# A convolution of three taps by points: inputs laid out ahead, output kept transposed, and the transform of x done channel block by channel block with two points of two output blocks among it

## The chip, the core and the metric

The kernel runs on one core of a Trainium2 chip. The metric is the device time of one execution in microseconds. It has four compute engines that run beside each other: TensorE (PE; its weight loads are shown as PEld), VectorE (DVE), ScalarE (ACT) and GpSimd (POOL). SyncE (SP) issues most of the DMA transfers here. TensorE writes into PSUM, of which there are eight banks of 512 fp32 values per partition; VectorE and ScalarE read it.

## The reference

x is (2, 2048, 1024), w is (3, 1024, 1024), all in bf16; the four parameters have 1024 values each.

```python
xp = jnp.pad(x, ((0, 0), (P, P), (0, 0)))          # P = 1
y = sum(jnp.einsum('bsc,cd->bsd', xp[:, k:k + S, :], w[k]) for k in range(K))   # K = 3
inv_std = 1.0 / jnp.sqrt(var + 1e-5)
y = (y - mean) * (g * inv_std) + b
return _silu(y)
```

It is a convolution along the sequence with three taps, a full product over 1024 channels for each tap, a batch norm with given mean and variance, and a silu.

## The kernel before, in words

Both kernels compute six neighbouring rows of the output from eight rows of the input by way of eight points (0, three pairs of plus and minus, and infinity). Per batch the 2048 rows make NB = 342 groups of R = 6. Three things have to be made from the data: the transform of x, called T (for each batch, channel block of 128 and point a tile of 128 channels x 342 groups), the transform of the weights (for points 1 to 6, the tiles u; points 0 and infinity use taps 0 and 2 of the weights as they are), and, for each batch and each of the eight output blocks of 128 channels, eight products of 8 matmuls each, which are then combined to six output rows.

**Transform of x.** x comes in as windows of 128 rows by 1024 channels (`load_x`, L119; 17 a batch, overlapping by two rows; 21 groups to a window, 6 in the last). TensorE multiplies a window's 128 channels with the matrix rm (L322): the result is already transposed, channels on partitions, 8 points x 21 groups = 168 columns. A job (`t_job`, L314) does up to three channel blocks of two windows into two PSUM banks, and one eviction casts the 1008 (or 672) columns a partition to bf16 in T (ScalarE L333 or VectorE L335). There are 24 such jobs a batch and one small one. At build time a small cost model (`clock`, `cost`, L106) gives each eviction to the engine that it thinks will end sooner. Batch 0's jobs run first, with four pairs of banks in turn (`ahead`, L604); batch 1's jobs are put between the matmuls of the first unit (class `Between`, L622), on the pairs at banks 4, 6 and 1.

**Units.** A unit is one output block of one batch (class `Unit`, L344). It holds four banks, 0 to 3 or 4 to 7, in turn. `run` (L473) issues the products of points 1, 3, 2, 4, 5, 6 (L369); after products 1, 3, 2 and 5 ScalarE copies a bank out (L380, L382), on which the next product into that bank waits; VectorE combines PSUM and the copies (L387). The products of point 0 and of infinity need nothing but T and the raw taps and are added onto two of the banks at the end. They (`first`, L400, `last`, L405) and the silus (L394) of one unit run inside the next one, behind its fifth and its sixth product (`rest`, L465, and the hook `behind`, L477). 16 units, dc by dc and batch by batch; the last one is done in two halves of the columns, 214 and 128 groups.

**Weights.** GpSimd adds and subtracts (L188, L167, L243), VectorE or ScalarE make the multiples by 2 and 4 (L169, L155, L237); `prepare_first`, `prepare_second` and `prepare_w` (L206, L230, L190) for output blocks 0, 1 and the others. The loads take 128 or 256 columns of a row of w at a time (L139).

**Matrix and parameters.** rm is made by some twenty small VectorE instructions (L77 to L102), the parameters are loaded as rows and transposed by TensorE (L282), and GpSimd makes scale and beta of them (L285 to L295).

**Output.** The silus leave yT, channels on partitions. `turn` (L572) sends it through a DMA transpose on SP and `store` (L581) writes rows of 128 channels. For the last two units TensorE transposes instead (`put`, L519, L530), VectorE or ScalarE copy out of PSUM (L531).

Each DMA on SP's queue waits for the eighth before it to have landed; a load into a tile waits also for its last reader.

Of the kernel before, what the change touches and what calls it, by code (L numbers as in the profile page):

```python
# [12 lines left out]
I32 = mybir.dt.int32  # L13
ENG = mybir.EngineType

P = 128
R = 6
NJ = 8
W0_AT = (5, 8, 16)
EARLY = 23  # L20
XBUFS = 12
T_FIRST = 21500.0
WARM = 2
WT = 21

@with_exitstack
def kernel(
    ctx: ExitStack,
    tc: tile.TileContext,
    x: bass.AP,  # L30
    w: bass.AP,
    mean: bass.AP,
    var: bass.AP,
    g: bass.AP,
    b: bass.AP,
# [3 lines left out]
    B, S, C = x.shape  # L39
    D = w.shape[2]  # L40
    CT, DC = C // P, D // P
    NB = -(-S // R)
    NW = -(-NB // WT)
    LAST = NB - WT * (NW - 1)
    assert S % P == 0 and NB <= 512
# [3 lines left out]
    wpool = ctx.enter_context(tc.tile_pool(name="wpool", bufs=1))  # L49
# [7 lines left out]
    opool = ctx.enter_context(tc.tile_pool(name="opool", bufs=2))  # L57
    xwin_scope = ExitStack()
    xpool = xwin_scope.enter_context(tc.tile_pool(name="xpool", bufs=XBUFS))
# [8 lines left out]
    rows = consts.tile([4 * DC, P], BF16, name="rows")  # L68
# [8 lines left out]
    def transform_matrix():  # L77
        v = nc.vector
        val = consts.tile([P, 3, WT], I32, name="val")
        nc.gpsimd.iota(val, pattern=[[1, 3], [-R, WT]], base=-1, channel_multiplier=1)  # L80
        m = consts.tile([P, 4, 3, WT], FP32, name="m")
        f = consts.tile([P, 3, 2, WT], FP32, name="f")
        c = consts.tile([P, 2, WT], FP32, name="c")
        rm = consts.tile([P, NJ, WT], BF16, name="rm")
        m0, m2, m4, m6 = (m[:, q] for q in range(4))
        for q, coef in ((1, -8.0), (2, 1.0), (3, 1.0), (0, 36.0)):
            v.tensor_scalar(m[:, q], val, float(2 * q), coef, op0=ALU.is_equal, op1=ALU.mult)
        for k, (c4, c6) in enumerate(((34.0, -8.0), (40.0, -32.0), (10.0, -2.0))):
            v.scalar_tensor_tensor(out=f[:, k], in0=m4[:, 1:3], scalar=c4, in1=m2[:, 1:3], op0=ALU.mult, op1=ALU.add)
        v.scalar_tensor_tensor(out=c, in0=m6[:, 0:2], scalar=-36.0, in1=m0[:, 0:2], op0=ALU.mult, op1=ALU.add)  # L90
        for k, (c4, c6) in enumerate(((34.0, -8.0), (40.0, -32.0), (10.0, -2.0))):
            v.scalar_tensor_tensor(out=f[:, k], in0=m6[:, 1:3], scalar=c6, in1=f[:, k], op0=ALU.mult, op1=ALU.add)
        v.scalar_tensor_tensor(out=c, in0=m4[:, 0:2], scalar=189.0, in1=c, op0=ALU.mult, op1=ALU.add)
        f1, f2, f3 = (f[:, k] for k in range(3))
        for j, a0, s0, a1, op in (
            (1, f1[:, 0], 1.0, f1[:, 1], ALU.add), (2, f1[:, 0], 1.0, f1[:, 1], ALU.subtract),
            (3, f2[:, 1], 2.0, f2[:, 0], ALU.add), (4, f2[:, 1], -2.0, f2[:, 0], ALU.add),
            (5, f3[:, 0], 2.0, f3[:, 1], ALU.add), (6, f3[:, 0], 2.0, f3[:, 1], ALU.subtract),
            (0, m2[:, 1], 23.625, c[:, 1], ALU.add), (7, m2[:, 0], -23.625, c[:, 0], ALU.subtract),
        ):  # L100
            v.scalar_tensor_tensor(out=rm[:, j], in0=a0, scalar=s0, in1=a1, op0=ALU.mult, op1=op)
        return rm  # L102

    rm = transform_matrix()

    clock = {"pe": 3500.0, "act": 0.0, "dve": 0.0, "dma": 3600.0}  # L106
    cost = {"act": (0.833, 250.0), "dve": (1.042, 215.0)}
    bank_free = {}

    def ends(e, size):  # L110
        return max(clock[e], clock["pe"] + 100.0) + cost[e][0] * size + cost[e][1]

    def busy(e, size):
        clock[e] = ends(e, size)

    order = [NW - 1] + list(range(2, NW - 1)) + [0, 1]
    xwin = {}

    def load_x(bi, wi):  # L119
        xw = xpool.tile([P, C], BF16, name="xw")  # L120
        lo = max(R * WT * wi - 1, 0)
        hi = min(lo + P, S)
        nc.sync.dma_start(out=xw[0:hi - lo, :], in_=x[bi, lo:hi, :])  # L123
        clock["dma"] += 5.4 * (hi - lo)
        xwin[bi, wi] = xw, clock["dma"]

    w_all = w.rearrange("k (ct p) d -> p k ct d", p=P)
    raw, wts = {}, {}

    wpools = {0: wpool}  # L130

    def load_w(pair, k, half=None):

        if (pair, "tile") not in raw:
            raw[pair, "tile"] = wpools[pair % 2].tile([P, 3, CT, 2, P], BF16, name=f"wch{pair % 2}")
        wch = raw[pair, "tile"]
        h0, h1 = (0, 2) if half is None else (half, half + 1)
        cols = slice((2 * pair + h0) * P, (2 * pair + h1) * P)
        nc.sync.dma_start(  # L139
            out=wch[:, k, :, h0:h1].rearrange("p c h d -> p c (h d)"), in_=w_all[:, k, :, cols]  # L140
        )
        clock["dma"] += 1400.0 * (h1 - h0)
        for h in range(2):
            raw[2 * pair + h] = wch[:, :, :, h]
# [200 lines left out]

# [382 lines left out]
```

## Time and profile before

| what | value |
|---|---|
| time, median of 3 runs | 187.73 us (187.33 to 187.81) |
| span of the profiled execution, first to last instruction | 185.5 us |
| time of the profiled execution beside its span | not given on the page |
| PE, DVE, ACT, POOL busy | 178.0, 153.0, 112.9, 146.8 us |
| products (L369) | 1088 matmuls: 960 of 342 columns, 64 of 214, 64 of 128 |
| windows of x (L322) | 272 matmuls, 256 of 168 columns |
| first window matmul, first product | 5.2 us, 19.6 us |
| last window matmul starts | 37.2 us |

How to read it: the page lists each engine's busy time, the span in 40 slices of 4.64 us, the chain of work that ended last, and the costliest groups of instructions. A group's line has the source line, the engine, what is written and read, the shape, the count, then busy microseconds and the mean length of one in nanoseconds, then the idle time ahead of them and who ended it. "L369" is a line of the kernel above. In the timeline and the chain, the first number is the start from the beginning of the span and the second the length, in microseconds.

### The profile page before, as it was taken

To read this page: it belongs to the slowest core of one execution; us is meant where nothing else is said; L and a number is where in the kernel's file an instruction comes from. 1 tells how busy PE (TensorE), PEld (TensorE's weight loads), DVE (VectorE), ACT (ScalarE), POOL (GpSimd) and SP (SyncE) were. 2 spreads that over 40 slices of the span, in tenths; PEclk is the share of its full clock that TensorE was granted. 3 is DMA by queue.
4 is the path that set the end of the run, shared out by engine and by line. 5 is a ranking of instruction groups with operands and counts; after the bars stand their busy time and mean duration, and the time that the engine had idled before them with its cause. 6 is when DMAs were issued, how large, how long until landed. Compare 5 with 4: busy or idle time off the path is not lost.

```text
span 185.5 us, 3732 instructions
## 1 busy us (share of the span) xinstructions
PE 178.0 (96%) x1403; PEld 125.9 (68%) x1403; DVE 153.0 (82%) x214; ACT 112.9 (61%) x183; POOL 146.8 (79%) x89
## 2 busy tenths in 40 slices
PE   6889999999999999999999999999999999999991
PEld 2678688866666666666666666666666666669890
DVE  5278777997668999999988998879988997678792
ACT  3589888896638565456545654565456546363791
POOL 7099899999998879999999999999999973020120
PEclk9999999999999999999999999999999999999998
DMA  5999999065426855698859557995583968766845
GB/s 166 326 344 328 377 386 252 7 203 143 79 48 62 183 106 134 198 200 187 161 114 206 109 135 156 217 211 108 136 178 80 209 57 203 151 139 134 196 96 113
DMA packets 88046, 31.72 MB, mean 171 GB/s; under 512 B 75659, under 2 KB 83866, under 8 KB 88028
## 3 DMA queue, kind: packets, MB, share of 16 engines
q1 hardware_dynamic: 86860, 31.24, 72.3%
q10 hardware_dynamic: 848, 0.20, 0.5%
q8 instruction: 11, 0.18, 0.4%
q0 software_dynamic: 320, 0.03, 0.2%
q14 instruction: 7, 0.06, 0.1%
HBM read 14.82 MB, written 8.39 MB: 125 GB/s over the span
## 4 chain that ended last, share of the span: by engine, by line
PE 85%; DMA 5%; DVE 4%; ACT 2%; SPq 1%; issue 0%; DVEq 0%; ACTq 0%
PE ps L369 79%; DMA xw<-in_x_dram 5%; PE ps L322 5%; DVE T_sb L335 3%; SPq L123 1%; ACT T_sb L333 1%; PE ps L530 1%; DVE sd L387 0%; DVE o L531 0%; ACT outer L394 0%; DVEq L335 0%; ACTq L333 0%
## 5 line engine op out<-in xcount | busy, mean ns | idle before, releaser
L369 PE MATMUL ps<-T_sb,u 128*128 128x342 bf16 (+2 forms) x816 | 120.1, 299 | 0.1
L369 PEld LDWEIGHTS <-u 128*128 128x128 bf16 x816 | 76.8, 97 | 33.4 <-issue 0.2
L188 POOL TENSOR_TENSOR u<-e,w1x 128x1024 bf16<-128x1024 f32 x32 | 69.4, 2191 | 3.9 <-DVE e L169 2.5
L369 PE MATMUL ps<-T_sb,wch 128*128 128x342 bf16 (+2 forms) x272 | 42.6, 299 | 0.4 <-ACT T_sb L333 0.4
L394 ACT ACTIVATE yT<-ps,beta,scale 128x342 bf16<-128x342 f32 (+4 forms) x49 | 33.5, 713 | 13.3 <-PE ps L369 13.3
L387 DVE SCALAR_TENSOR_TENSOR t<-ps,sd 128x684 f32<-128x684 f32 (+2 forms) x51 | 39.1, 822 | 0.6
L188 POOL TENSOR_TENSOR u<-e,wch 128x1024 bf16<-128x1024 f32 x16 | 38.5, 2424 | 1.2 <-DMA wch<-in_w_dram 0.7
L369 PEld LDWEIGHTS <-wch 128*128 128x128 bf16 x272 | 25.7, 97 | 11.9 <-issue 0.6
L380 ACT COPY pc<-ps 128x342 f32<-128x342 f32 (+2 forms) x35 | 14.9, 426 | 28.7 <-PE ps L369 28.4
L333 ACT CAST T_sb<-ps 128x1008 bf16<-128x1008 f32 (+2 forms) x31 | 25.6, 874 | 7.4 <-PE ps L322 7.1
L335 DVE CAST T_sb<-ps 128x1008 bf16<-128x1008 f32 (+2 forms) x19 | 20.7, 1116 | 10.4 <-PE ps L322 10.3
L387 DVE SCALAR_TENSOR_TENSOR ps<-ps,t 128x684 f32<-128x684 f32 (+2 forms) x34 | 28.3, 832 | 0.6
L169 DVE SCALAR_TENSOR_TENSOR e<-wch 128x1024 f32<-128x1024 bf16 x12 | 26.2, 2182 | 0.0
L322 PE MATMUL ps<-rm,xw 128*128 128x168 bf16 (+2 forms) x272 | 25.0, 237 | 1.0 <-ACT T_sb L333 0.3
L322 PEld LDWEIGHTS <-xw 128*128 128x128 bf16 (+2 forms) x272 | 20.9, 100 | 6.4 <-issue 3.7
L387 DVE SCALAR_TENSOR_TENSOR ps<-ps,pc 128x342 f32<-128x342 f32 (+2 forms) x34 | 16.9, 497 | 9.2 <-PE ps L369 7.8
L167 POOL TENSOR_TENSOR e<-wch 128x1024 f32<-128x1024 bf16 x7 | 16.9, 2409 | 0.4 <-DMA wch<-in_w_dram 0.4
L394 ACT ACTIVATE yT<-t,beta,scale 128x684 bf16<-128x684 f32 (+2 forms) x17 | 15.7, 924 | 0.0
L387 DVE SCALAR_TENSOR_TENSOR t<-ps,t 128x684 f32<-128x684 f32 (+2 forms) x17 | 13.9, 818 | 0.0
L589 POOL DMA_DIRECT2D out_dram<-o x2 | 1.3, 659 | 15.6 <-DMA o<-yT 15.6
L387 DVE SCALAR_TENSOR_TENSOR sd<-pc,ps 128x342 f32<-128x342 f32 (+2 forms) x17 | 8.2, 485 | 6.2 <-ACT sd L380 6.1
L380 ACT COPY sd<-ps 128x342 f32<-128x342 f32 (+2 forms) x17 | 7.3, 428 | 9.7 <-PE ps L369 9.1
(62 smaller groups left out, 61.8 us busy)
## 6 DMA issues: line engine op xcount, KB each, us to landing
xw<-in_x_dram SPq DMA_DIRECT2D x32, 256.0 KB
out_dram<-o SPq DMA_DIRECT2D x28, 192.0 KB
wch<-in_w_dram SPq DMA_DIRECT2D x8, 512.0 KB
wch<-in_w_dram SPq DMA_DIRECT2D x8, 256.0 KB
out_dram<-o SPq DMA_DIRECT2D x14, 120.0 KB
out_dram<-o SPq DMA_DIRECT2D x3, 128.0 KB
o<-yT SPq DMA_TRANSPOSE x15
out_dram<-o SPq DMA_DIRECT2D x12, 7.5 KB
```

The costliest lines, as they stand in the source:

```text
L123: nc.sync.dma_start(out=xw[0:hi - lo, :], in_=x[bi, lo:hi, :])
L167: eng.tensor_tensor(e, w0, w2, op=ALU.add)
L169: eng.scalar_tensor_tensor(out=e, in0=f, scalar=4.0, in1=h, op0=ALU.mult, op1=ALU.add)
L188: nc.gpsimd.tensor_tensor(wts[dc, q][:, i], sums[dc, q], o, op=(ALU.add, ALU.subtract)[i])
L322: nc.tensor.matmul(v[:, q, c], lhsT=xw[0:rows, (c0 + c) * P:(c0 + c + 1) * P], rhs=mat[0:rows, :, 0:n], start=True, stop=True,)
L333: nc.scalar.copy(dst, src)
L335: nc.vector.tensor_copy(dst, src)
L369: nc.tensor.matmul(self.bank[q], lhsT=lhsT, rhs=T_sb[self.bi][:, ct, j, nsl], start=not add and ct == 0, stop=ct == CT - 1, skip_group_che ...
L380: nc.scalar.copy(dst, self.bank[q])
L387: nc.vector.scalar_tensor_tensor(out=out, in0=in0, scalar=scalar, in1=in1, op0=ALU.mult, op1=op1)
L394: nc.scalar.activation(dst, src, ACT.Silu, bias=beta[:, dc:dc + 1], scale=scale[:, dc:dc + 1])
L530: nc.tensor.transpose(v[:, a, q], src, ident)
```

## The change

The host now lays out the inputs: x as windows by channel block, (batch, block of 128 channels, 128 rows, 16 windows, 128 channels), and the rest of its rows apart (xl, 48 rows); w as (output block, 128 rows, tap, channel block, 128 columns); the parameters as columns; and the matrix rm as an input. The output is stored as it lies in yT (output block, channel, 6, 342), and the host reorders it. The building of rm, the transpose of the parameters, the DMA transposes (`turn`), the transposes by TensorE (`put`), and one of two warming matmuls are gone.

T is made channel block by channel block: a load brings one block of all 16 windows (512 KB), and its three jobs are six, six and four windows. The jobs of both batches take the pairs of banks at 4 and 6 in turn. Banks 0 to 3 hold, during batch 0's transform, the sums of points 0 and infinity for output blocks 0 and 1 of batch 0: as soon as the cost model thinks that a channel block of T is complete, its matmuls are issued among the jobs. These four sums are copied to SBUF (`ends_of`), and units 0 and 2 add them in on VectorE (two more instructions each) in place of the two products; their silus, three of 684 columns, go to places 1, 2 and 3 of the following unit. Batch 1's jobs are again put between the matmuls of the first unit, whatever is left behind its fifth product (`between.rest`). The cost model has new constants.

In the order that results, 23 of batch 0's 24 large jobs are evicted by ScalarE and one by VectorE; of batch 1's, 21 and three. Behind the first unit's fifth product there are 13 jobs left, all for ScalarE.

```diff
-T_FIRST = 21500.0
-WARM = 2
+AHEAD = 2
+XBUFS = 8
...
-    for _ in range(WARM):
-        nc.tensor.matmul(ps[:, 7], lhsT=zeros[:, 0:P], rhs=zeros, start=True, stop=True)
+    nc.tensor.matmul(ps[:, 7], lhsT=zeros[:, 0:P], rhs=zeros, start=True, stop=True)
...
-    rm = transform_matrix()
+    rm = consts.tile([P, NJ, WT], BF16, name="rm")
+    nc.scalar.dma_start(out=rm, in_=rm_in)
...
-    cost = {"act": (0.833, 250.0), "dve": (1.042, 215.0)}
+    cost = {"act": (0.833, 60.0, 200.0), "dve": (1.042, 160.0, 60.0)}
...
+    class Jobs:
+        def __init__(self, bi, banks):
+            self.bi, self.banks, self.n = bi, banks, 0
+            self.todo = [(None, 0, 0)] + [
+                (ct, f, min(6, NF - f)) for ct in range(CT) for f in range(0, NF, 6)
+            ]
...
+        def do(self):
+            clock["pe"] = max(clock["pe"], self.ready())
+            bank = self.banks[self.n % len(self.banks)]
+            self.n += 1
...
+                src = ps[:, bank:bank + 2, 0:per * NJ * WT].rearrange("p b (f j n) -> p b f j n", f=per, j=NJ)
+                for q in range(nf):
+                    nc.tensor.matmul(
+                        src[:, q // per, q % per], lhsT=xt[self.bi, ct][:, f + q], rhs=rm, start=True, stop=True
+                    )
+                src = src.rearrange("p b f j n -> p j b f n")
+                dst = T[:, ct, :, f * WT:(f + nf) * WT].rearrange("p j (b f n) -> p j b f n", b=2, f=per)
+            clock["pe"] += size / 2.3
+            e = min(("act", "dve"), key=lambda k: ends(k, size, clock["pe"]))
...
         def rest(self, between, last=5, first=6):
+            if self.ends is not None:
+                return [
+                    (1, lambda: self.silu(slice(2, 4), self.y23)), (2, lambda: self.silu(slice(0, 2), self.low)),
+                    (3, lambda: self.silu(slice(4, 6), self.high)),
+                ]
...
-            self.combine(sd[:, 1], pa, 2.0, b3, ALU.subtract)
+            self.combine(sd[:, 2], pa, 2.0, b3, ALU.subtract)
+            s0 = s5 = sd[:, 0:3:2]
+            if self.ends is not None:
+                self.combine(sd[:, 1], b3, 1.0, self.ends[:, 0])
+                self.combine(sd[:, 3], sd[:, 2], 1.0, self.ends[:, 1])
+                s0, s5 = sd[:, 1:3], sd[:, 0:4:3]
...
+    jobs = Jobs(0, (4, 6))
+    accs = [(dc, k, bank) for dc, k, bank in ((0, 0, 0), (0, 2, 3), (1, 0, 1), (1, 2, 2)) if dc < AHEAD]
...
+    while jobs or any(todo.values()):
+        best = ahead()
+        if jobs and (best is None or jobs.ready() <= max(clock["pe"], best[0])):
+            ct, f, nf = jobs.todo[0]
+            jobs.do()
+            if ct is not None and f + nf == NF:
+                complete.add((0, ct))
+        else:
+            ahead_do(best)
...
     class Between:
+        jobs = Jobs(1, (4, 6))
...
+        if i == 0:
+            second[0]()
+            also = also + [(5, between.rest)]
+        if i == 1:
+            also = [(1, second[1]), (2, second[2]), (4, second[3])] + also
...
+    h1 = Unit(dc, bi, 0, 0, H)
+    h1.run(quiet, [(3, h0.silu_inner)])
+    h0.store(sp, inner)
+    h0.product(3, NJ - 1, True, quiet)
+    h0.product(0, 0, True, quiet)
+    h1.product(0, 0, True, quiet)
+    h1.product(3, NJ - 1, True, quiet)
```

More of the change, by code (lines that the diff above doesn't have):

```diff
@@ L12 @@
 BF16 = mybir.dt.bfloat16
-I32 = mybir.dt.int32
 ENG = mybir.EngineType
@@ L127 @@
[L127 to L144, printed above, removed]
@@ L344 @@
+    yts = [ypool.tile([P, R, NB], BF16, name=f"yT{q}") for q in range(B)]
     class Unit:
@@ L677 @@
-    before.store(late)
+            second[0]()
+            also = also + [(5, between.rest)]
+        if i == 1:
+            also = [(1, second[1]), (2, second[2]), (4, second[3])] + also
+        if i == 3:
+            also = also + [(1, lambda: idle(act_work)), (1, lambda: idle(dve_work))]
+        if i == len(seq) - 2:
+            also = prev.rest(quiet, 4, 5)
+        unit.run(
+            between if i == 0 else quiet, also,
+            2 if i == 2 else dc + 2 if bi == 1 and 0 < dc < DC - 2 else None, i == 2,
+        )
@@ L705 @@
[L705 to L709 removed]
+    inner, outer = slice(1, R - 1), slice(0, R, R - 1)
+    h0 = Unit(dc, bi, 4, H, NB)
+    h0.run(quiet, prev.rest(quiet, 5, 5))
+    prev.store(sp)
+    h1 = Unit(dc, bi, 0, 0, H)
[4 more added lines that the diff above has]
+    h1.product(0, 0, True, quiet)
```

611 lines of the change are left out of this document (229 added, 382 removed), and 8 rows, old and new, of the table _POINTS.

## The prediction

> **What bounds the kernel now.** I read the page's parts 1 and 2 first, then the busy time by stretches, then the chain of work that ended last in order of time, then the groups by shape.
>
> ```profile
> PE 178.0 (96%) x1403; PEld 125.9 (68%) x1403; DVE 153.0 (82%) x214; ACT 112.9 (61%) x183; POOL 146.8 (79%) x89
> ...
> PEclk9999999999999999999999999999999999999998
> ...
> GB/s 166 326 344 328 377 386 252 7 203 143 79 48 62 183 106 134 198 200 187 161 114 206 109 135 156 217 211 108 136 178 80 209 57 203 151 139 134 196 96 113
> ```
>
> TensorE is busy 96% of the span, but a matmul's recorded time overlaps the next one, so this does not say that it issues all the time. The chain does:
>
> ```profile
> 30.27 1.22 DVE T_sb L335
> 31.49 0.04 issue
> 31.54 0.61 PE ps L322 x6
> 32.15 0.02 issue
> 32.17 1.21 DVE T_sb L335
> ...
> 37.44 136.02 PE ps L369 x952
> ...
> 180.47 0.46 PE ps L369 x8
> 180.93 0.03 issue
> 180.95 0.57 ACT outer L394
> 181.53 0.42 DVE o L531
> ```
>
> Columns: start, length, what. Two things are to be seen. From 37.44 on TensorE is the bound: 952 products in 136.02 us. 32 of them have 214 columns (0.0918 apart), which leaves 133.1 for 920 of 342 columns, **0.1447 each**. Before that the chain alternates between an eviction and the next transform: eviction over, 0.05 later six matmuls into the PSUM banks it freed (0.61), 0.02 later the eviction of those. This loop prices the change. TensorE's whole work is 1024 products of 342 columns (148.2) and the transforms (256 windows at 0.0725, 18.6, and small ones), some 167 us; the rest of the span is the wait for the first data, the waits before 37.44, and the tail.
>
> **Durations** come from the groups by shape (count, busy us and mean ns):
>
> ```profile
> L333 ACT CAST T_sb<-ps 128x1008 bf16<-128x1008 f32 x17 | 17.0, 1007 | 3.6 <-PE ps L322 3.4
> L333 ACT CAST T_sb<-ps 128x672 bf16<-128x672 f32 x13 | 9.5, 731 | 0.3 <-PE ps L322 0.2
> L335 DVE CAST T_sb<-ps 128x1008 bf16<-128x1008 f32 x15 | 17.9, 1206 | 9.0 <-PE ps L322 8.9
> L530 PE MATMUL ps<-ident,yT 128*128 128x128 bf16 x34 | 2.9, 219 | 0.0
> ```
>
> and from ScalarE's timeline:
>
> ```profile
> 37.18 1.62 ACT L333 CAST T_sb<-ps 128x1008 bf16<-128x1008 f32 x2
> ...
> 40.20 1.06 ACT L155 ACTIVATE w1x<-wch 128x1024 bf16<-128x1024 bf16 x1
> 41.16 0.45 ACT L382 ACTIVATE pc<-ps 128x342 f32<-128x342 f32 x1
> ...
> 46.15 0.95 ACT L394 ACTIVATE yT<-t,beta,scale 128x684 bf16<-128x684 f32 x1
> 47.00 0.91 ACT L394 ACTIVATE yT<-ps,beta,scale 128x684 bf16<-128x684 f32 x1
> 47.94 0.44 ACT L380 COPY pc<-ps 128x342 f32<-128x342 f32 x1
> ```
>
> The first line is a 1008 eviction and a 672 one, 1.62 together. The 672 row gives the second 0.72, so it starts 0.90 after the first began, though the first is over only after 1.00. In the same way the next instruction starts 0.61 after a 672, 0.35 after a copy of 342, 0.96 after a scaled weight (40.20 to 41.16), 0.85 or 0.94 after a silu of 684 from SBUF or PSUM.
>
> **Phase 1, the transform of batch 0.** Before, its 24 large jobs take four pairs of banks in turn, and both engines evict (over both batches ScalarE 31, VectorE 19 jobs). In the changed program, banks 0 to 3 hold the sums of points 0 and inf, so jobs have two pairs (4-5, 6-7), and its order gives all large jobs but one to ScalarE. A channel block is three jobs, A and B (1008) and C (672). Set C's eviction at 0. A reuses the pair that B left: B began 0.90 earlier and is over at 0.10; 0.05 and 0.63 later A's eviction starts, 0.79, where ScalarE was free at 0.61. B starts 0.90 after A (1.69), the next C at 2.58. So **2.58 us per block**, 20.6 for eight. The first A starts at about 4.7: the old first window starts at 5.2 behind two warming matmuls (3.78 us, half of which go), and then the first half block, 0.36 MB at the first slice's pace, sets it; 0.5 either way. The last C is over at 25.3. The 32 early products (0.145 each) fit into TensorE's waits, except the last four, behind that eviction: 26.0. The loads do not set this: 5.6 MB, of which the page's row moves 0.77 in the first slice and, at the 385 GB/s of its best slices, the rest by 17.2.
>
> **Phase 2, batch 1 with the first unit.** Till all but 13 jobs are done TensorE issues 40 products (5.8), 64 window matmuls (4.64) and 8 small ones (0.3), and is the bound: 36.7 to 36.8. Then all remaining jobs (a C and four blocks) come in one run, all on ScalarE, which begins that C at 38.1 behind a copy: 38.1 + 4 x 2.58 = 48.4 for the last C. TensorE has issued its last window at 47.8, does the first unit's sixth product (1.16), and starts the second unit at **48.9**.
>
> **What is left then.** 880 products of 342 columns (127.3), and the last unit in two column halves: 64 at 0.0918 (5.9) and 64 at 0.0559 (3.6), starts read off the trace: 136.8, so **185.7**. In the old trace this remainder begins at 42.1 (37.44 and 32 products more), with 37 transposes of 0.056 in it (2.1 us of TensorE), which the change drops. So the changed kernel is 6.8 late there and gets 2.1 back.
>
> **Pile-ups on ScalarE in units 1 and 3.** The change takes the two early products out of units 0 and 2, which so far ran inside the following unit behind its fifth product, and puts three silus of 684 there, in units 1 and 3, at ScalarE's first free places. Unit 1 has also three scaled weights ahead of its last copy. From its first copy at 50.3: 0.35, 0.96, 0.85, 0.36, 0.96, 0.94, 0.35, 0.94, 0.96, and 0.44 for the copy that its sixth product waits on: 57.4, where TensorE came to it at 54.7. Loss **2.7**. In unit 3 the same with one scaled weight: its fourth product waits 0.6 for a copy, and the sixth 0.7, since no product stands between it and the copy of the fifth: **1.3**. GpSimd does not add: its chain for block 1 (2.13 a step) is ready 1 to 2 us ahead of each product. Bounds of this part: 0, if silus and copies came in a kinder order, and 5.2, if the silus also delay VectorE's sums by the length of one more silu.
>
> **Tail.** The second half's products take 0.45 each, its first copy waits for the unit before's silus, and its sixth product for two silus of the first half: 1.2. After the last product four silus stand on ScalarE (two of 256, two of 128 columns), of which 1.6 lies behind it; then a store. The old trace gives 3.3 from its last eviction (182.2) to the end, and I take that. The old tail was 4.6 behind the last product (180.9).
>
> **Hidden edits.** Parameters and matrix by DMA, one warming matmul less, and larger DMA pieces end before the first eviction loop does; if that cover went, they are worth at most the 1.9 us of one warming matmul. The loads of batch 1 wait for TensorE to free each tile, a block behind the transform; each load is 1.4 us against 2.58 a block, so none is late. Stores from the transposed output replace 15 DMA transposes; both run beside products, and a store waits for silus already done. The old end's copies and transposes off TensorE are in the tail's sums.
>
> **The sum.** 185.7 + 2.7 + 1.3 + 1.2 + 1.6 + 3.3 = 195.8, against a span of 185.5: +10.3. The page gives the profiled execution's span alone; the median of the three times is 2.2 above it, and I carry that over: 187.7 + 10.3 = **198.0 us**. Unknown: the eviction in its new order of elements (runs of 126 instead of 42). The nearest rows are ScalarE's own 1007 ns, which I take, and VectorE's 1206 for the same size; a tenth less would give some 2 us back, a fifth more would cost some 6. With the start and the pile-ups this makes 191.5 to 202.
>
> **Rivals.**
> *Faster: evictions keep pace with the loads.* The place is the wait of a job for its pair of banks. If a job needed 0.65 us instead of 0.86, the 48 jobs would give back the 10.3; below that the change wins. At the old pace (25 evictions of batch 0 from 5.7 to 20.2, 0.58 each) phase 1 ends at 20, phase 2 is TensorE's 16.7, and the sum is 36.7 + 136.8 + 5.2 + 4.9 = 183.6: 185.8 us. For it: TensorE's first window can start sooner, and transfers grow: of 88046 packets 75659 are under 512 B. Against it: two pairs stand in the program, and no row shows a 1008 eviction under 1.00.
> The Trainium skill (DMA: Bandwidth & Descriptors, Specifications) asks for at least 512 B per transfer, which speaks for this rival; the trace agrees in so far as the slices with split weights move 326 to 344 GB/s and those of whole rows 377 to 386.
> *Pile-ups hidden, the loop as forecast:* 198.0 - 5.2 = 192.8.
> *TensorE's clock falls in the gaps.* In the old trace the first window matmuls (16 from 5.78 in 1.91 us) start 0.14 apart and later ones 0.0725. If the gaps of phase 1 (TensorE issues 14.5 of 21 us) and of the run of 13 jobs (5 of 11) bring the slow pace back, a job's matmuls take 1.08 instead of 0.63, 0.21 more per job over two pairs, 48 jobs: 10 us, 208. Against it: no gap in my sum is over 1.3 us, and the old phase 1 issued 9.9 of 14.5 us at the full clock.
> The Trainium skill (TensorE: Matmul & The Clock Gate, Part 1) puts the fall to half clock behind an idle window of about 3.4 us; by that it does not happen here.
>
> **How the numbers follow.** Forecast 0.66; pile-ups hidden 0.15; faster 0.11; clock 0.05; gains and losses cancelling 0.03. About 0.3% is what a measurement of this kernel can tell from no change, so faster 0.11, same 0.03, slower 0.86. The range leaves out the faster rival and the clock: 189.5 to 202.5.
>
> **What would show it.** Right: ScalarE busy without a gap from 5 to 25 and 38 to 49, VectorE nearly idle there; transform evictions 2.58 per three; PE waits on ScalarE of about 0.6 per block; the second unit's first product at 49; waits of 2.7 in it; slices 2 to 10 of TensorE visibly below the rest. Wrong: all transforms done before 42, or the second unit without a wait.

## The result, and the profile after

The changed kernel takes 205.05 us (median of 4 runs, 204.31 to 205.99) where the kernel before takes 187.53 beside it: a ratio of 1.0944 [1.0894, 1.0993], the 95% interval in brackets. The profiled execution has a span of 203.9 us. The forecast was 198.0 with an upper end of 202.5, so the direction was right and the time lies outside the range.

From the page of the changed kernel, the busy time, the granted clock and the transfers in 40 slices of 5.1 us:

```profile
PE 179.6 (88%) x1362; PEld 125.6 (62%) x1362; DVE 134.4 (66%) x177; ACT 122.8 (60%) x191; POOL 141.0 (69%) x74
...
PEclk9999999999999999999999999999999999999995
...
GB/s 172 368 418 394 322 231 106 0 0 0 266 136 15 0 247 118 0 29 233 103 0 118 142 103 0 255 29 81 96 10 103 0 106 0 103 70 39 142 64 0
```

TensorE's busy time is what it was (179.6 against 178.0) in a span that is 18.4 longer, so its share falls from 96 to 88%. The loads of the first batch move faster than before (368 to 418 GB/s in slices 2 to 4). The chain of waits in order of time (start, length, what) shows both the loop that the forecast priced and the start that it did not:

```profile
2.58 5.77 DMA xw<-in_x_dram
8.35 0.05 issue
8.39 1.02 PE ps L259 x6
...
15.13 0.61 PE ps L259 x6
15.74 0.02 issue
15.76 1.91 ACT T_sb L271 x2
17.67 0.04 issue
17.71 0.61 PE ps L259 x6
18.32 0.02 issue
18.34 1.91 ACT T_sb L271 x2
...
37.36 1.36 DVE sd L313 x3
...
65.89 2.46 DVE sd L313 x3
```

From 15.76 to 18.34 a channel block takes 2.58 us, to the hundredth what the recurrence gave: two evictions, then six windows into the pair that they freed, then the next. Above it, the second block's windows wait for their load until 8.35, and six of them take 1.02 instead of 0.61: matmuls start 0.14 apart there. The row of the granted clock shows full there, but the trace's first record of that clock is at 14.4, which is where the slow pace ends. The evictions by shape:

```profile
L271 ACT CAST T_sb<-ps 128x1008 bf16<-128x1008 f32 x30 | 29.2, 1004 | 5.8 <-PE ps L259 5.1
L271 ACT CAST T_sb<-ps 128x672 bf16<-128x672 f32 x14 | 10.3, 736 | 1.2 <-PE ps L259 1.2
```

The new order of their elements costs nothing: 1004 and 736 ns against 1007 and 731. Last, the DMA issues (what, count, size, us from issue to landing), a line whose time the forecast took from the old kernel's stores:

```profile
out_dram<-yT SPq DMA_DIRECT2D x15, 513.0 KB, 7.8
```

Units are counted from 0, so unit 1 is the second.

| place in the span, us | forecast | measured |
|---|---|---|
| last eviction of batch 0 over | 25.3 | 28.6 |
| second unit's first product | 48.9 | 52.3 |
| waits in units 1 and 3 | 2.7, 1.3 | 2.4, 2.0 |
| wait at the tail | 1.2 | 0.86 |
| silus behind the last product | 1.6 | 1.5 |
| last silu over to end of span | 3.3 | 7.2 |
| span | 195.8 | 203.9 |

Of the 8.1 us beyond the forecast 3.4 are there when the second unit starts, 3.9 come behind the last silu, and 0.8 are spread between.

### The profile page after: what moved, and what is told of

It is laid out like the page before. It is cut to its first block, busy times and chain, and to the rows that moved or that the text cites. A ratio compares the mean times of both kernels' runs of the same rounds, so it can differ in the third digit from the quotient of the medians.

```text
span 203.9 us, 3449 instructions
## 1 busy us (share of the span) xinstructions
PE 179.6 (88%) x1362; PEld 125.6 (62%) x1362; DVE 134.4 (66%) x177; ACT 122.8 (60%) x191; POOL 141.0 (69%) x74
## 4 chain that ended last, share of the span: by engine, by line
PE 68%; ACT 16%; DVE 6%; DMA 3%; issue 3%; SPq 1%; DVEq 0%; ACTq 0%
PE ps L296 62%; ACT T_sb L271 10%; PE ps L259 6%; DMA xw<-in_x_dram 3%; ACT yT L318 3%; DVE sd L313 2%; DVE t L313 2%; ACT w1x L130 2%; DVE T_sb L273 1%; DVE ps L313 1%; ACT pc L306 1%; PE ps L439 1%; ACT sd L306 1%; SPq L104 0%; ACT pc L308 0%
## 5 line engine op out<-in xcount | busy, mean ns | idle before, releaser
L296 PE MATMUL ps<-T_sb,u 128*128 128x342 bf16 (+2 forms) x816 | 118.8, 299 | 4.6 <-ACT pc L306 3.2
L271 ACT CAST T_sb<-ps 128x1008 bf16<-128x1008 f32 (+2 forms) x45 | 38.5, 909 | 7.8 <-PE ps L259 6.3
L318 ACT ACTIVATE yT<-ps,beta,scale 128x342 bf16<-128x342 f32 (+4 forms) x48 | 33.3, 727 | 12.2 <-PE ps L296 12.2
L296 PE MATMUL ps<-T_sb,wch 128*128 128x342 bf16 (+2 forms) x240 | 36.7, 298 | 0.0
L259 PE MATMUL ps<-rm,xw 128*128 128x168 bf16 x256 | 29.3, 254 | 8.3 <-ACT T_sb L271 5.3
L259 PEld LDWEIGHTS <-xw 128*128 128x128 bf16 x256 | 22.7, 105 | 15.3 <-issue 10.1
L296 PEld LDWEIGHTS <-wch 128*128 128x128 bf16 x240 | 22.6, 97 | 9.8
L147 DVE SCALAR_TENSOR_TENSOR e<-wch 128x1024 f32<-128x1024 bf16 x12 | 25.7, 2143 | 0.0
L141 POOL TENSOR_TENSOR e<-w1x,wch 128x1024 f32<-128x1024 bf16 x4 | 8.5, 2124 | 17.4 <-ACT w1x L130 17.2
L141 POOL TENSOR_TENSOR e<-wch 128x1024 f32<-128x1024 bf16 x8 | 19.2, 2404 | 1.7 <-DMA wch<-in_w_dram 1.7
L273 DVE CAST T_sb<-ps 128x1008 bf16<-128x1008 f32 (+2 forms) x5 | 4.7, 936 | 12.3 <-PE ps L259 12.0
```

The costliest lines, as they stand in the source:

```text
L141: nc.gpsimd.tensor_tensor(sums[dc, q], a, b, op=ALU.add)
L147: nc.vector.scalar_tensor_tensor(out=e, in0=f, scalar=4.0, in1=h, op0=ALU.mult, op1=ALU.add)
L259: nc.tensor.matmul(src[:, q // per, q % per], lhsT=xt[self.bi, ct][:, f + q], rhs=rm, start=True, stop=True)
L271: nc.scalar.copy(dst, src)
L273: nc.vector.tensor_copy(dst, src)
L296: nc.tensor.matmul(self.bank[q], lhsT=lhsT, rhs=T_sb[self.bi][:, ct, j, nsl], start=not add and ct == 0, stop=ct == CT - 1, skip_group_che ...
```

## The experiments

Two theories stand at the head. **A**: the loss is the turn of two pairs of PSUM banks, with the loads' landing and the stores' landing on top. **B**: it is ScalarE's rate alone, and the banks are second. Each ratio is against the kernel before, run beside it on the same chip; the changed kernel's own was 1.0944 and, run again with others, 1.0900. "First phase ends" is the end of batch 0's last eviction.

**Rows of the output further apart** (768 bytes instead of 684; the host drops the padding).

```diff
-_OUTS = [((2, 8, 128, 6, 342), "bfloat16")]
+_OUTS = [((2, 8, 128, 6, 384), "bfloat16")]
```

> Only the output tensor changes: 384 groups a row in memory instead of 342 (768 bytes a row instead of 684), so that each row starts at a multiple of 256 bytes; the 42 extra are never written. In the changed kernel the last packets move at 198.4 us of the span and the two last stores count as landed at 202.5 and 202.8, some 4 us later; in the kernel before 256-byte pieces at whole multiples of 256 land about 1 us after their last packet. Theory A (pieces that start in the middle of a block of memory are confirmed late): the last stores land 1 to 1.5 us after their last packet, span 200.5 to 201.5, time 202 to 202.5. Theory B (the lateness belongs to stores out of this tile or this amount, wherever the pieces start): last landing still 4 us late, time 205, within 0.5.

Measured: 201.12 us, ratio 1.0734 [1.0691, 1.0776], span 199.9. The end of the span comes 4.6 us behind the last product instead of 8.7. Its DMA issues:

```profile
out_dram<-yT SPq DMA_DIRECT2D x15, 513.0 KB, 3.6
```

In the changed kernel the last data packet is over at 198.26 and the last landing is at 202.77, 4.5 later; here 198.42 and 198.85. So the stores were not slow to move but late to be confirmed. The gain is as theory A expected, and somewhat larger (202 to 202.5 expected); by what feature of the layout is taken up below.

**Two engines on two pairs** (the middle job of each block on VectorE).

```diff
-            e = min(("act", "dve"), key=lambda k: ends(k, size, clock["pe"]))
+            e = "act" if ct is not None and f != 6 else "dve"
```

> Job B of each channel block (six windows, 1008 columns) is evicted by VectorE, A and C by ScalarE; the two pairs of banks stay. Theory A (a pair of banks is held 0.63 for the matmuls, 0.05 and the eviction, so two pairs allow a job per 0.84 us whoever evicts): a block takes 2.4 to 2.5 us instead of 2.58, time 203.5 (1 to 2 us less). Theory B (ScalarE's own rate sets the block: 0.90 + 0.90 + 0.61): without B ScalarE needs 1.5 a block, the transform follows the loads in phase 1 and TensorE in phase 2, time 192 to 195.

Measured: 208.94, ratio 1.1116 [1.1050, 1.1183]: 4 us worse than the changed kernel, where B expected a gain and A a small one. With two pairs the first phase keeps a period of 2.54 per block (the windows of its blocks start at 14.03, 16.43, 19.14, 21.53, 24.18), though ScalarE has a third less to do: the middle job's eviction lies in the loop with 1.21 instead of a step of 0.90. So the two pairs bind by themselves. In the second phase TensorE waits 2.06, 1.87 and 0.65 us (from 37.1, 41.3 and 44.2), the first two times for evictions that stand behind the first unit's combines in VectorE's queue, and then its chain shows this:

```profile
44.33 1.22 DVE T_sb L273
45.55 0.04 issue
45.59 1.85 PE ps L259 x12
47.44 0.03 issue
```

Twelve windows take 1.85 us; in the first phase the same twelve (14.03) issued at 0.0725 apart. They start 0.14 apart from 45.7 to 54, and the granted clock in this trace is 0.50 from 45.3 to 55.6. This is the rival "clock falls in the gaps", which the forecast gave 0.05: it did not happen in the changed kernel's second phase, and it did here.

**Four single banks instead of two pairs, both engines, and ScalarE alone.** The same four banks, but jobs of three (or two) windows into one bank each.

```diff
-                (ct, f, min(6, NF - f)) for ct in range(CT) for f in range(0, NF, 6)
+                (ct, f, nf) for ct in range(CT) for f, nf in ((0, 3), (3, 3), (6, 3), (9, 3), (12, 2), (14, 2))
...
-            e = min(("act", "dve"), key=lambda k: ends(k, size, clock["pe"]))
+            e = "act" if self.n % 5 in (0, 2, 4) else "dve"
...
-    jobs = Jobs(0, (4, 6))
+    jobs = Jobs(0, (4, 5, 6, 7))
```

> Single banks as in e3a, and of five jobs two go to VectorE. Theory A (both limits have to go): a block 1.4 to 1.6 us; batch 0's transform ends with the loads, at 21 to 23 instead of 28.6, the 13-job run of phase 2 (here twice as many half jobs) takes 6 to 7 us instead of 11, time 193 to 196. Theory B of e2 and of e3a would have shown these times there already.

Measured: 199.18, ratio 1.0615 [1.0568, 1.0662], half of what was expected: the first phase ends at 24.0 instead of 28.6, but in the second TensorE waits 2.35 us at 38.4 behind VectorE's combines, and issues windows 0.14 apart from 41.5 to 44.8, at a granted clock of 0.50.

> A job is three windows (504 columns, or two with 336) in one bank, four banks (4 to 7) in turn instead of two pairs; all evictions are ScalarE's. So PSUM holds the same amount but is given back in smaller pieces. Theory A (the pairs and ScalarE's rate lie at nearly the same height): ScalarE's rate remains, 4 x 0.47 + 2 x 0.32 = 2.5 us a block, time 203 to 205. Theory B (the pairs alone set the block): a block falls to TensorE's and the loads' 1.2 to 1.5 us, time 192 to 195.

(In this kernel the engine is always ScalarE.) Measured: 204.1, ratio 1.0891 [1.0847, 1.0934], level with the changed kernel. ScalarE evicts 19 of these jobs in 8.21 us without a gap, 2.59 for the six of a block. So neither alone helps: two pairs give 2.54 to 2.58 with either choice of engines, ScalarE alone 2.59 with any banks. Theory B is half of the cause and so is A; both have to go together.

**No early points, four pairs in the first phase.**

```diff
-AHEAD = 2
+AHEAD = 0
...
-    jobs = Jobs(0, (4, 6))
+    jobs = Jobs(0, (0, 2, 4, 6))
```

> The points 0 and inf of the two output blocks go back into their units (32 products, 4.6 us, out of the first phase), and the first phase's window results turn over four pairs of PSUM banks instead of two, so its evictions can fall on both engines. Theory A (the first phase is set by the turn of two pairs on one engine, 2.58 us per block): the first phase ends 2 to 3 us behind the last landing, at 21 to 22 instead of 28.6; the added products lie beside the second batch's evictions in the first unit, and only the third unit is longer for them (2.3 us), so about 4 us less than the changed kernel, 200 to 202. Rival B (the first phase is set by its loads and by TensorE's half rate at the start, the banks are second): it ends at 26 or later, and with 2.3 us of products back in the third unit the time is 205 to 208.

Measured: 197.13, ratio 1.0526 [1.0504, 1.0547], more than theory A expected. The first phase ends at 22.0; the second unit starts at 44.5 instead of 52.3; from there 256 products run without a wait of 0.1 us, where the changed kernel loses 2.4 and 2.0 in units 1 and 3. Less 32 products that are back in units 1 and 3 (4.6) this makes 7.8 + 4.4 - 4.6 = 7.6, and the last product ends 7.6 earlier (187.6 against 195.2); 0.9 more is gained behind it. Its waits of TensorE (us in total, times, longest):

```profile
PE ps L259 <- DMA xw<-in_x_dram: 4.2, 5, 2.2
PE ps L259 <- ACT T_sb L271: 4.1, 10, 0.5
```

The loads now head the list in the first phase, which the forecast's faster rival had wanted. Behind the wait of 2.2 the granted clock is 0.50 from 8.7 to 12.2, and windows issue 0.14 apart there.

**Three small parts of the changed kernel, one at a time**: the silus of units 0 and 2 at place 5 of the next unit; x blocks 1 and 2 loaded ahead of the weights' taps; matmuls of zeros behind the first block's jobs, whose result is not used.

```diff
-                    (1, lambda: self.silu(slice(2, 4), self.y23)), (2, lambda: self.silu(slice(0, 2), self.low)),
-                    (3, lambda: self.silu(slice(4, 6), self.high)),
+                    (5, lambda: self.silu(slice(4, 6), self.high)), (5, lambda: self.silu(slice(0, 2), self.low)),
+                    (5, lambda: self.silu(slice(2, 4), self.y23)),
```

> The silus of the two units whose points 0 and inf come early are moved from the places 1 to 3 of the following unit to its place 5. Theory A (the waits of 2.45 us in the second unit and 1.65 in the fourth are ScalarE's queue: three double silus ahead of the point copies): both waits shrink to under 0.5 each, 2 to 3.5 us less than the changed kernel, 201.5 to 203. Rival B (the second unit's wait is what is left of the 13 evictions in a run, and not the silus): under 1 us less, 204 to 205.

```diff
 load_x(0, 0, 2)
-load_w(0, (0,))
 load_x(0, 1)
-load_w(0, (2,))
 load_x(0, 2)
+load_w(0, (0,))
+load_w(0, (2,))
```

> The second and third channel blocks of x are loaded ahead of the two weight taps. Theory A (the first phase is a chain of evictions from its first block on, so what its second block's windows wait for, 8.35 instead of some 7.6, is paid in full at its end): 0.5 to 1 us less than the changed kernel, 204 to 204.5. Rival B (the late start is taken up by the weights' taps, which the early products and GpSimd's sums then wait for): 205 or more.

```diff
+            if self.bi == 0 and ct in (None, 0):
+                for _ in range(4 if ct == 0 and f == 12 else 1):
+                    nc.tensor.matmul(ps[:, 2], lhsT=zb[:, 0:P], rhs=zb, start=True, stop=True)
```

> Matmuls of zeros on 512 columns into a bank not yet used follow the first block's window jobs, so that TensorE has no idle stretch before the second block's windows come; they compute nothing that is used. Theory A (the half rate of the windows until 12.9 us comes of TensorE's idle time, and each of the first blocks' six windows at 1.0 instead of 0.61 us is paid in the chain): the six windows at 8.4 and after take 0.61, and the first phase ends 0.8 to 1.5 us earlier, 203.5 to 204.3. Rival B (the rate at the start goes by the time since the launch or by something else than idle time): still 1.0 until about 12.9, 205 or more.

Measured: 203.77, 203.87 and 204.38, ratios 1.0882 [1.0847, 1.0917], 1.0869 [1.0819, 1.0919], 1.0909 [1.0871, 1.0947]. None can be told from the changed kernel's second run (below). What the traces show:
- Silus moved: the excess over a product each 0.1447 apart is 0.72 in unit 1 instead of 2.44, but 1.43 in unit 2, which had none, 1.3 in units 3 and 4, and 0.9 in unit 5: some 4.4 in all, as before. From the second unit's first product to the last product it takes 142.8 us, against 142.9. The wait went to GpSimd's weights (1.2 us on `u`) and to VectorE. Theory A's 2 to 3.5 us did not come.
- Load order: the second block's windows start at 8.33, no earlier than in most other runs, since the first block's now start late. No gain.
- Zeros: the second block's windows start at 8.44, behind the last of the zeros, and twelve of them take 1.18 us, so they issue 0.07 apart at once, where the changed kernel is at 0.14 until 14. The idle time was the cause of the slow pace, as theory A says. The first phase ends at 27.1, 1.5 earlier than in the changed kernel, but only 0.2 and 0.3 earlier than in the two kernels beside it, whose slow pace ended by 11.2 and 10.4 without zeros. In the second phase 0.7 is lost again (24.4 against 23.7): VectorE's three sums, which stand ahead of an eviction there, take 2.07 instead of 1.36. So the time shows no gain.

**The changed kernel again, three pairs in the second phase, and all of it together.**

> The changed kernel once more, beside the next two and on their chip. In the profiled runs of one and the same first phase the second channel block's load was over at 7.65 to 8.50 us and the half rate ended between 8.4 and 13, so the last eviction of the first phase was over between 27.1 and 28.6. If that is chance of the run, it lies in that stretch again and the time is 203.7 to 205.1; if it is a matter of the kernel, the phase ends at 28.6 as in the first run.

Measured: 204.79, ratio 1.0900 [1.0865, 1.0936]; the first phase ends at 28.4. The three kernels above, with nearly the same first phase, end it at 27.1 to 27.4; all others that leave it as it is, at 27.8 to 28.8. In the kernel with the silus moved nothing differs before 27, so 27.3 to 28.8, some 1.5 us, is the chance of the run or of the chip: there the second block's windows start at 7.70 and the slow pace ends at 11.2. The changed kernel's 28.6 is 0.2 above the middle of the nine runs with this first phase (28.4), so little of its late start is chance.

```diff
-        jobs = Jobs(1, (4, 6))
+        jobs = Jobs(1, (4, 6, 1))
...
-            also = also + [(5, between.rest)]
+            also = also + [(4, between.rest)]
```

> One part of the changed kernel is altered: the second batch's jobs take three pairs of banks (4-5, 6-7, 1-2), and those left go ahead of the first combine into bank 1, behind the first unit's fourth product, where VectorE is still free of combines. Theory A (13 evictions in a run on ScalarE at 2.58 us per block set the second unit's start): the second unit starts at 46 to 48 instead of 51 to 52, the waits in units 1 and 3 stay (about 4 us), 4 to 5 us less than the changed kernel, 199 to 201. Rival B (the second phase is bound by the loads of the second batch, or by GpSimd's weights for the first unit): the second unit starts at 50 or later, 203 to 205.

Measured: 201.75, ratio 1.0747 [1.0714, 1.0781]. The second unit starts at 49.5, from a first phase that ends at 28.6 as before: 2.8 us gained of the 4 to 5 expected. From the first phase's end this is 20.9, against 23.7. TensorE's own work there is 17.2 (128 windows at 0.0725, 48 products at 0.1447, 0.3 of small ones, 0.7 of early products), so 3.7 us of waits stay with three pairs.

For the combination, the three edits above for rows, early points and pairs are made at once, and the tail has one more:

```diff
-    h1.run(quiet, [(3, h0.silu_inner)])
+    h1.run(quiet, [(5, h0.silu_inner)])
```

> All that was found to cost is taken out at once: output rows at a pitch of 768 bytes, no early points, four pairs in the first phase and three in the second, and the first half's inner silus of the last unit one step later. Theory A (the losses are those of the turn of the banks, the pile-ups, the late confirmation of the stores and the tail's wait, and they add up): span 195.4 with four pairs and no early points, less 4 for the stores, 3 to 5 for the second phase, 0.8 for the tail: 186 to 188, a time of 187.5 to 189.5, level with the kernel before or up to 1% above it. Rival B (the second batch's loads or the weights end last once the banks do not): 191 or more.

Measured: 190.71, ratio 1.0164 [1.0139, 1.0189], span 188.6: between the two theories. The losses add up nearly as expected; 14 of the 17.5 us are gone with these four causes, and the kernel before stays faster by 1.6%.

**An even spread, and early points of one block.** The paced kernel is the combined one with the second batch's jobs spread over the first unit's products, the middle job of a block on VectorE, and the tail's silus in another order.

```diff
-            if self.jobs and self.jobs.ready() <= clock["pe"]:
-                self.jobs.do()
+            self.calls += 1
+            while self.jobs and 30 * self.jobs.n < 25 * self.calls:
+                self.jobs.do()
...
+            if self.bi:
+                e = "dve" if f == 6 else "act"
...
-    h0.silu(outer, ps[:, h0.b0:h0.b0 + 4:3, H:NB])
-    h1.silu_inner()
+    h1.silu_inner()
+    h0.silu(outer, ps[:, h0.b0:h0.b0 + 4:3, H:NB])
```

> The combined kernel again, with three things changed: the second batch's jobs are spread evenly over the first unit's first 32 products and none is left for a run; VectorE evicts the middle job of each of its blocks and ScalarE the other two; and at the tail the last half's inner silus go ahead of the other half's outer ones. Theory A (what is left against the kernel before is the run of seven ScalarE evictions from 31.9 to 38.4 and the waits of 0.8, 0.9 and 0.5 us around it): the second unit starts at 38 to 39 instead of 40.3, the tail is 0.3 to 0.6 shorter, time 188 to 189. Rival B (the second batch's last block lands at 30.7 and jobs issued evenly wait for their loads): no gain, 190.5 or more.

Measured: 190.54, ratio 1.0177 [1.0137, 1.0216]: no gain, though not for rival B's reason. The run of ScalarE evictions is gone, and the same loop has formed with VectorE (chain):

```profile
28.84 1.22 DVE T_sb L275
30.06 0.04 issue
30.10 0.59 PE ps L259 x6
```

Three jobs a block over three pairs give the middle job the same pair each time: its eviction, then its next windows, 1.22 + 0.04 + 0.59 + 0.02, some 1.9 per block. The second unit's first product is at 41.7, against 41.4 in the combined kernel (the 40.3 of the expectation is the first unit's sixth product).

```diff
-AHEAD = 2
+AHEAD = 1
...
-    jobs = Jobs(0, (4, 6))
+    jobs = Jobs(0, (4, 6, 1))
```

> The changed kernel with early points for the first output block alone: banks 0 and 3 hold them, and the first phase's jobs turn over three pairs of banks; the second phase is as in the changed kernel. Theory A (the early points lose by the banks that they take, not by themselves): the first phase ends at 22 to 24 instead of 27 to 28.6 though 16 early products stay in it, the second unit's wait of some 2 us stays, the fourth unit's goes, second unit from 46 to 48, 198.5 to 201. Rival B (the early products themselves hold up the windows behind them, or the loads do): the first phase ends at 26 or later, 203 or more.

> The paced kernel with early points for the first output block on three pairs of banks, and its silus at place 5 of the following unit. Theory A (16 early products, 2.3 us, fit into TensorE's idle time in the first phase, which is some 6 us there, and the price is one wait of about 1 us in a later unit): 1 us less than the paced kernel. Rival B (three pairs are too few for the first phase, or the waits in the second and third unit come to 2.3 us or more, 1.7 in the run with the silus moved): level with the paced kernel or up to 1.5 us more.

Measured: 199.34 for the first, ratio 1.0628 [1.0604, 1.0653]: the first phase ends at 23.7 with 16 early products in it, the second unit starts at 46.5, and the fourth unit's wait is gone: theory A. The second, which is the paced kernel with one block's early points on three pairs, takes 194.91, ratio 1.0388 [1.0365, 1.0411], 4.2 us of span more than without them: rival B, and beyond it. Its first phase ends at 24.3 instead of 21.8, and unit 2 again waits 1.2 for its weights. The chain has a loop of 2.0 per block there:

```profile
21.46 0.87 DVE T_sb L275
22.32 0.04 issue
22.37 0.32 PE ps L441
22.69 0.74 PE ps L259 x10
23.43 0.02 issue
```

An early product (L441) stands in it between the eviction that frees a pair and the ten windows that want it; it puts them off by 0.16 (the 0.32 is its recorded length, which the windows overlap). So the early products cost on both accounts, by the pair that they take and by standing ahead of windows. Together with what hangs on them, one block's come to more than the 2.3 us that they save: 2.5 more in the first phase, 2.0 more from its end to the second unit (the last two early products and their copies stand ahead of the first unit, and VectorE's two added sums ahead of an eviction), and 2.1 of waits in units 1 and 2.

**What makes the stores land late.** The pitch of the rows alone is changed; these times are of one execution each.

```diff
-_OUTS = [((2, 8, 128, 6, 342), "bfloat16")]
+_OUTS = [((2, 8, 128, 6, 368), "bfloat16")]
```

> The changed kernel with output rows 736 bytes apart (multiples of 32). If the late confirmation comes of pieces that share a stretch of 64 bytes with their neighbours (684 bytes apart does), it is as with 684: stores land 7 to 8 us after their issue, span 202.5 to 204. If any pitch above the row's length will do, since neighbours then never touch the same bytes' row, 3.6 us and a span near 200.

> The same with rows 704 bytes apart (multiples of 64). Theory 64: whole stores land 3.6 us after their issue, as at 768, and the span is near 200. Theory 256 (a row must start on a multiple of 256): 7 to 8 us, span 202.5 to 204.

> The same with rows 896 bytes apart (multiples of 128, every other one of 256). Theory 64: 3.6 us and a span near 200. Theory 256: half of the rows start off the multiples, and one late row is enough for the whole store: 7 to 8 us, span 202.5 to 204.

Measured: spans of 199.4, 199.8 and 199.1, whole stores landing 4.4, 4.5 and 3.6 us behind their issue. The theory of the first run, that a row must start on a multiple of 256 bytes, falls as the main cause: 736 and 704 do nearly as well (4.4 and 4.5, against 3.6 with 768 and 896). The last run leaves rows 684 apart and sets the channels 4788 bytes apart instead of 4104:

```diff
-_OUTS = [((2, 8, 128, 6, 342), "bfloat16")]
+_OUTS = [((2, 8, 128, 7, 342), "bfloat16")]
```

> Rows stay 684 bytes apart and abut as in the changed kernel, whole-unit pieces stay 4104 bytes long, but each channel has room for a seventh row, so that channels lie 4788 bytes apart instead of 4104. Theory row (rows that abut, or start on odd multiples of 4 bytes, are confirmed late): stores land 7 to 8 us after their issue, span 202.5 to 204. Theory channel (the distance of 4104 bytes from channel to channel, 8 more than 4096, is what makes the confirmation late; the pitches of 704 to 896 changed it to 4224 to 5376): 3 to 4.5 us and a span near 200.

Measured: 202.54, span 200.8, in one execution. Its DMA issues:

```profile
out_dram<-yT SPq DMA_DIRECT2D x15, 513.0 KB, 2.7
```

This is the fastest of all. Eleven runs that leave the output's layout as it is have 6.7 to 7.8 there, so the place of the channels makes a whole store late by 4 to 5 us. In the changed kernel a late whole store's last packet has moved 3.9 to 4.9 us before it lands (the last seven); here it is 0.3 to 0.6. The end comes 6.0 us behind the last product, against 7.1 to 8.7 in those eleven runs and 4.6 where the rows too lie further apart.

What this run does not tell: with 4788 bytes the channels' pieces also no longer abut, as rows and channels do not with 704 to 896. So the distance of 4104 by itself (that it is close to 4096 is only a guess) and the abutting of neighbouring pieces are both left as the cause. That the tail stays partly late here, where the last unit's rows still abut, speaks for the second; no run with abutting channels at another distance was made.

## Why the prediction was wrong, point by point

- **The loop per channel block: right.** 2.58 forecast, 2.58 measured, from rows of the old trace alone, in both phases. The second phase took 23.7 where 23.6 was forecast.
- **"The loads do not set this" and the start of the chain: wrong, 3.3 us.** The step counted bytes at the best slices' rate and asked when the last load ends; it is the second block's load that stops the chain (8.35). The step also priced every window at 0.0725 from the first block on, and put at nothing the half pace of the first windows that the old trace shows. In the changed kernel windows issue 0.14 apart until 14.4, because TensorE had idled; with zeros in the idle time the first phase ended 1.5 earlier. By place: the first large eviction starts at 5.2 instead of 4.7 (within the 0.5 given), and the first evictions of the next three blocks follow 1.7, 0.9 and 0.2 later than 2.58 apart. The forecast's own sentence, "no gap in my sum is over 1.3 us", is off too: TensorE's gap at 7 is 1.45.
- **"Then a store. The old trace gives 3.3 ... and I take that": wrong, 3.9 us.** The stores' addresses are part of the change, and the row taken is from a store with another layout. 3.3 should have been a lower bound with an open upper end: the eleven runs with this layout have 5.6 to 7.2 there. With the measured 7.2 in its place the forecast is 201.9; with the late start alone it is 201.4. Either would lie inside the range, so it took both misses to leave it.
- **Pile-ups: right in cause in unit 1, the sum partly luck** (2.7 + 1.3 forecast, 2.4 + 2.0 measured). In unit 3 the silu ahead of the late copy waits 0.60 (until 73.39) for VectorE, which has run without a gap since its three sums at 65.89. What was not foreseen either: moving the silus only moves the wait, to GpSimd's weights and to VectorE.
- **Tail wait and silus: right** (1.2 and 1.6 against 0.86 and 1.5).
- **VectorE's added work** was costed at nothing. It lies in the chain twice, at 37.36 and at 65.89 (1.36 and 2.46 us for three sums, two of them added, one of which reads SBUF alone). That last sum takes 0.50 where GpSimd is idle or just done, but 1.61 in unit 2 and 2.38 in the kernel with two engines: each time longer than 0.51 it ends 0.37 behind the GpSimd instruction that was running as it began, while the sum that reads PSUM takes 0.51 beside GpSimd too. No run took the added sums out by themselves, so their share of the waits is not known.
- **"32 of them have 214 columns": a miscount.** The 952 products hold 40 of them, which makes the others 0.1451 apart; over 880 products this is 0.4 of the 0.8 us that are spread between.
- **Rivals.** The faster one needed the loads to set the pace; they do so as soon as there are four pairs and two engines, and even then the kernel is 5% slower than before. The clock rival came true in two experiments after waits of about 2 us in the second phase, and in a third in the first phase (after 2.20). The Trainium skill (TensorE: Matmul & The Clock Gate, Part 1) puts the fall behind an idle window of about 3.4 us; the trace agrees in the length, since the half clock lasts 3.41, 3.41 and 10.24 us (three times 3.41), but not if the window means a single gap, since none of the waits ahead (2.06, 1.87 and 0.65 in one run, 0.80 and 2.35 in another, 2.20 in the third) is as long.

What stays open: 1.6% between the combined kernel and the one before. Its second unit starts at 41.4, where the old kernel has issued as many products by 37.3; 1.0 of that is from the first phase (21.2 against 20.2) and 3.1 from the second. From there to the last product 1.0 comes back (142.6 us against 143.6, which has transposes in it), and the tail behind the last product is as long (4.6 in both). A spread that changes pair and engine from block to block was not tried.

## What to carry to other kernels

Price an eviction loop by two limits at once, what the engine needs per block and what one pair of banks needs for windows, hand-over and eviction, and expect no gain from lifting only one; banks given to accumulators that are wanted later are taken from that loop. Where a change moves the addresses of a store, the landing time of the old store is no row for it: leave the end of the span open above. The sum over a start should be made load by load, since a chain of evictions pays for its first late block in full.

## What the runs showed of the hardware

- Stores of 513 KB whose 128 channels lie 4104 bytes apart, and so abut, land 7.8 us behind their issue (6.7 to 7.8 over eleven runs), and 2.7 with 4788 bytes, the pieces being 4104 bytes long in both. Their packets had moved by then: the last packet of the span is over 4.5 us ahead of the last landing in the changed kernel and 0.43 ahead with rows 768 apart. The Trainium skill (DMA: Bandwidth & Descriptors, Specifications) asks for at least 512 bytes a transfer; by that these stores are well formed, and the trace shows that length was not what counted.
- Windows issued 0.14 instead of 0.0725 apart for some 8 us after TensorE had waited 4.6 of 7.8 us in three gaps, the longest 2.06, and the granted clock reads 0.50 there for 10.24 us. It reads 0.50 for 3.41 us behind a wait of 2.20, and behind two of 0.80 and 2.35. A single wait of 1.95 (the paced kernel with one block's early points, until 41.2) did not bring it.
- A VectorE sum of 342 columns with both tensors in SBUF waits for the running GpSimd instruction: it took 0.50 us without one and 0.71 to 2.38 beside one, and ended 0.37 or 0.38 behind it in all 22 cases (14 runs) where it was longer than 0.51. With one tensor in PSUM the same sum took 0.51 beside GpSimd.
